# Transposing queries into (row, neighbour) order so that an output tile stores as one DMA

## The chip, the cores and the metric

The kernel runs on one core of a Trainium2 chip. The metric is the device time of one execution in microseconds (us). Each kernel was run several times beside the kernel before on the same chip. PE is the matrix engine, DVE the vector engine, ACT the scalar engine, POOL the GpSimd engine, and SP the engine that issues nearly all DMAs here.

## The reference, cut to what matters

Eight batches of 576 tokens and 8 heads of 64 go through two attentions (32 packed queries gather from k and v; then every token attends to the 32 packed rows), and the result through a two-layer block with a squared ReLU.

```python
def _attn_ref(q, k, v, p):
    p_packed = sm_attn(p, k, v)            # (8, 8, 32, 64)
    return sm_attn(q, p_packed, p_packed)  # (8, 8, 576, 64)

def _moe_ref(x, w_in, w_out):              # x: 4608 tokens x 512
    r = np.maximum(x @ w_in, 0.0)          # d_ff = 2048
    return (r * r) @ w_out                 # 4608 x 512, float32
```

One thing about checking: in the reference's own output the spread among the rows of one batch is below 1e-10 beside a typical value of 2.2e-5, because the inputs are small and the second softmax is nearly uniform. A kernel that stores rows in exchanged places therefore still compares as correct. Where an order of rows is called right below, that rests on the index arithmetic, not on the comparison.

## The kernel before

The 576 tokens of a batch are written as s = 18·a + j, with a = 0..31 (the row) and j = 0..17 (the neighbour). A load puts (head, a) on the partitions and (j, d) in the free dimension, so each partition reads one long run. DVE transposes blocks of 32 x 32; the columns of `qT`, which are the tokens from here to the end, come out in the order (j, a).

```python
def tr_q(self, qd):
    self.tile_of("qT", att, [P, NQD, 2, S], BF16, bufs=1)
    nc.vector.transpose(
        self.qT[:, qd].rearrange("p dh (j a) -> p j dh a", a=32),
        self.t.qb[qd][:].rearrange("p (j dh dl) -> p j dh dl", dh=2, dl=32))
...
def n_mul(self, qd, hf):           # softmax weights times 1/sum, on DVE
    nc.vector.tensor_tensor(out=self.a2[:, qd, n0:n1]..., in0=self.e2[qd, hf], in1=self.rs[qd, hf], op=ALU.mult)
...
def f2_out(t, eng):                # 128 tokens of output, t = 0..35
    ob[t] = opool.tile([P, NE], F32, name="o_sb")      # 3 buffers
    cast(eng, ob[t], po[t])
    for i in range(4):
        b, j = divmod(t * 4 + i, JT)                   # JT = 18
        dst = out[b * S:(b + 1) * S, :].rearrange("(a j) e -> j a e", j=JT)[j]
        nc.sync.dma_start(dst, ob[t][32 * i:32 * i + 32, :])
```

A tile of 128 tokens is four j of 32 rows each, so it is stored by four DMAs of 32 runs of 2 KB.

The softmax here doesn't subtract the row's maximum and nothing guards it: scores larger than these inputs give would overflow.

## Time and profile before

| | before |
|---|---|
| time on the chip, first three runs | 274.54 us median (274.21 to 275.49) |
| span of the profiled run | 271.4 us |
| PE / DVE / ACT / POOL busy | 243.0 / 172.7 / 168.6 / 82.7 us |
| stores | 144 of 64 KB, 1.7 us from issue to landing |

From the profile's page, kernel before: busy time of two engines, the 40 slices of DVE and PE, the DMA packets by size, and the chain that ended last.

```profile
PE 243.0 (90%) x1840; PEld 135.4 (50%) x1840; DVE 172.7 (64%) x325; ACT 168.6 (62%) x302; POOL 82.7 (30%) x127
...
PE   0436967999989999999999999999999999999992
...
DVE  4756799999949899859768974976266504510000
...
DMA packets 31129, 46.99 MB, mean 173 GB/s; under 512 B 10113, under 2 KB 18305, under 8 KB 31105
...
PE ps_o L636 31%; PE ps_h L612 17%; DVE gT L627 6%; DMA v_f<-in_v_dram 4%; DMA kq_f<-in_k_dram 4%; DMA out_dram<-o_sb 3%; DVE qT L455 3%; PE ps_a L542 3%; PE ps_s L572 3%; SPq L645 3%; PE ps_a L473 2%; DVE a L600 2%; PE ps_pp L507 2%; DVE M L552 2%; ACT o_sb L340 1%
```

Each digit of the slices is a busy share in tenths over 6.8 us. DVE is full from slice 6 to 11, PE nearly so from slice 8 on. The same as a table by stretches of time (start:end, length, then busy us and number of instructions of PE, weight loads, DVE, ACT, POOL, the PE clock that the chip granted as a share of full speed, the DMA share and GB/s):

```profile
55.00:76.00 21.00, 19.85 (x119) 11.34 (x117) 21.00 (x29) 12.19 (x21) 13.07 (x16) 1.00 1.03 260
76.00:105.00 29.00, 28.71 (x269) 15.65 (x268) 23.86 (x45) 22.15 (x44) 20.05 (x37) 1.00 0.96 271
105.00:150.00 45.00, 44.88 (x396) 27.11 (x396) 35.88 (x71) 36.09 (x67) 18.05 (x28) 1.00 0.68 193
150.00:200.00 50.00, 50.00 (x415) 28.37 (x413) 33.15 (x69) 37.40 (x69) 5.22 (x4) 1.00 0.28 73
```

From 55 to 76 us DVE has no idle time at all; after it PE has next to none, while DVE is idle for a fifth to a third.

The groups of transposes by shape (count, busy us, mean ns of one, idle before): the query transpose, and the two of the keys.

```profile
L455 DVE STREAM_TRANSPOSE qT<-q_b 128x1152 bf16<-128x1152 bf16 x16 | 21.4, 1358 | 0.4 <-ACT q_b L340 0.4
L461 DVE STREAM_TRANSPOSE kT<-k_b 128x1024 bf16<-128x1024 bf16 x16 | 19.8, 1235 | 5.7 <-PE ps_a L487 4.8 <-POOL k_b L342 0.6
L464 DVE STREAM_TRANSPOSE kT<-k_b 128x128 bf16<-128x128 bf16 x16 | 4.3, 269 | 0.0
```

From the two key transposes a column costs (1235 - 269) / (1024 - 128) = 1.08 ns, and one instruction about 0.13 us besides.

The end of the kernel: ACT's copy of the last tile and SP's four store issues.

```profile
266.65 0.59 ACT L340 COPY o_sb<-ps_o 128x512 f32<-128x512 f32 x1 [2.87 <-DMA out_dram<-o_sb]
267.26 1.73 SPq L645 DMA_DIRECT2D out_dram<-o_sb  x4
```

### The profile page before, as it was taken

Reading aid. Unit: us, or ns where it says so; the run is one execution under the profiler, and the core shown is the slowest. Engines: PE = TensorE matmul, PEld = TensorE weight load, DVE = VectorE, ACT = ScalarE, POOL = GpSimd, SP = SyncE. Lnnn points to the kernel's source line nnn. Section 1 sums busy time; section 2 is a strip of 40 time slices with the busy share of each in tenths; the row PEclk is TensorE's granted clock in tenths of the full one; section 3 lists DMA queues with packets and bytes.
Section 4 is the critical chain, followed back from the end, with each engine's and each line's share of the span. In section 5 each row is a group of like instructions: output and inputs, shape, how many; then the busy total and the mean of one; then the engine's idle time right before and its main releaser. Section 6 shows DMA issues by size and latency. Waiting matters only on the chain.

```text
span 271.4 us, 5108 instructions
## 1 busy us (share of the span) xinstructions
PE 243.0 (90%) x1840; PEld 135.4 (50%) x1840; DVE 172.7 (64%) x325; ACT 168.6 (62%) x302; POOL 82.7 (30%) x127
## 2 busy tenths in 40 slices
PE   0436967999989999999999999999999999999992
PEld 0322443456555544665565466556546646644441
DVE  4756799999949899859768974976266504510000
ACT  3436646867548798788868975976587717821110
POOL 5432338629589381362246213000000000000000
PEclk9999999999999999999999999999999999999997
DMA  7999999999897999807955911111111131113223
GB/s 258 230 310 398 270 319 386 358 261 334 176 291 236 259 330 239 332 1 168 328 173 119 280 41 40 41 39 42 39 41 39 39 77 41 40 50 76 73 74 77
DMA packets 31129, 46.99 MB, mean 173 GB/s; under 512 B 10113, under 2 KB 18305, under 8 KB 31105
## 3 DMA queue, kind: packets, MB, share of 16 engines
q1 hardware_dynamic: 30576, 46.55, 60.5%
q8 instruction: 14, 0.23, 0.4%
q10 hardware_dynamic: 528, 0.13, 0.2%
q14 instruction: 11, 0.08, 0.1%
HBM read 37.22 MB, written 9.44 MB: 172 GB/s over the span
## 4 chain that ended last, share of the span: by engine, by line
PE 60%; DVE 18%; DMA 11%; SPq 4%; ACT 2%; issue 2%; POOL 1%; DVEq 0%; POOLq 0%; ACTq 0%
PE ps_o L636 31%; PE ps_h L612 17%; DVE gT L627 6%; DMA v_f<-in_v_dram 4%; DMA kq_f<-in_k_dram 4%; DMA out_dram<-o_sb 3%; DVE qT L455 3%; PE ps_a L542 3%; PE ps_s L572 3%; SPq L645 3%; PE ps_a L473 2%; DVE a L600 2%; PE ps_pp L507 2%; DVE M L552 2%; ACT o_sb L340 1%
## 5 line engine op out<-in xcount | busy, mean ns | idle before, releaser
L636 PE MATMUL ps_o<-w_out_b,gT 128*128 128x512 bf16 x576 | 147.5, 379 | 0.4 <-DVE w_out_b L342 0.3
L620 ACT ACTIVATE r<-ps_h 128x576 bf16<-128x576 f32 x124 | 78.2, 651 | 26.6 <-PE ps_h L612 18.9
L627 DVE TENSOR_TENSOR gT<-r 128x576 bf16<-128x576 bf16 x128 | 71.1, 580 | 28.6 <-ACT r L620 27.7
L612 PE MATMUL ps_h<-a,M 128*128 128x288 bf16 x512 | 82.1, 292 | 2.2 <-DVE r L622 1.2
L636 PEld LDWEIGHTS <-gT 128*128 128x128 bf16 x576 | 54.6, 98 | 50.2 <-issue 4.4
L612 PEld LDWEIGHTS <-M 128*128 128x128 bf16 x512 | 49.7, 99 | 31.6 <-issue 6.1
L340 ACT COPY o_sb<-ps_o 128x512 f32<-128x512 f32 x29 | 17.0, 585 | 32.5 <-DMA out_dram<-o_sb 25.8
L550 ACT ACTIVATE M<-ps_a,rD 128x512 bf16<-128x512 f32 x39 | 26.4, 686 | 6.2 <-PE ps_a L542 5.8
L342 POOL CAST q_b<-kq_f 128x1152 bf16<-128x1152 f32 (+1 forms) x16 | 19.7, 1244 | 25.5 <-DMA kq_f<-in_q_dram 25.2
L342 POOL CAST v_b<-v_f 128x1280 bf16<-128x1280 f32 (+1 forms) x15 | 18.8, 1279 | 27.1 <-PE ps_pp L511 10.1
L461 DVE STREAM_TRANSPOSE kT<-k_b 128x1024 bf16<-128x1024 bf16 x16 | 19.8, 1235 | 5.7 <-PE ps_a L487 4.8
L342 POOL CAST k_b<-kq_f 128x1152 bf16<-128x1152 f32 (+1 forms) x15 | 17.7, 1180 | 13.5 <-DMA kq_f<-in_k_dram 9.4
L455 DVE STREAM_TRANSPOSE qT<-q_b 128x1152 bf16<-128x1152 bf16 x16 | 21.4, 1358 | 0.4 <-ACT q_b L340 0.4
L552 DVE TENSOR_SCALAR M<-ps_a,rD 128x512 bf16<-128x512 f32 x25 | 18.7, 747 | 4.4 <-PE ps_a L542 4.2
L473 PE MATMUL ps_a<-pT_bd,kT 128*128 128x128 bf16 x128 | 10.0, 230 | 11.0 <-DVE pT_bd L342 8.3
L542 PE MATMUL ps_a<-w_in_b,ppT 64*32 64x512 bf16 x256 | 16.8, 413 | 3.0 <-ACT M L550 1.1
L342 POOL COPY pT_bd<-pT 32x64 bf16<-32x64 bf16 x56 | 13.5, 267 | 10.9 <-PE ps_a L487 8.8
L473 PEld LDWEIGHTS <-kT 128*128 128x128 bf16 x128 | 8.6, 103 | 13.4 <-DVE kT L461 9.2
L579 ACT ACTIVATE e<-ps_s,rD 128x576 bf16<-128x576 f32 x16 | 11.4, 739 | 5.8 <-PE ps_s L572 5.7
L342 DVE CAST pq_bd<-ps_pp 32x64 bf16<-32x64 f32 x32 | 7.0, 218 | 11.2 <-PE ps_pp L511 5.9
L572 PE MATMUL ps_s<-qT,pq_bd 128*128 128x288 bf16 x64 | 11.0, 306 | 3.1 <-ACT pq_bd L340 1.8
L600 DVE TENSOR_TENSOR a<-e,rs 128x576 bf16<-128x576 bf16 x16 | 13.6, 848 | 0.0
(51 smaller groups left out, 145.0 us busy)
## 6 DMA issues: line engine op xcount, KB each, us to landing
kq_f<-in_k_dram SPq DMA_DIRECT2D x16, 576.0 KB, 8.2
kq_f<-in_q_dram SPq DMA_DIRECT2D x16, 576.0 KB, 7.1
out_dram<-o_sb SPq DMA_DIRECT2D x144, 64.0 KB, 1.7
v_f<-in_v_dram SPq DMA_DIRECT2D x28, 256.0 KB, 5.9
w_f<-in_moe_w_in_dram SPq DMA_DIRECT2D x8, 512.0 KB, 8.2
w_f<-in_moe_w_out_dram SPq DMA_DIRECT2D x8, 512.0 KB, 8.4
v_f<-in_v_dram SPq DMA_DIRECT2D x8, 128.0 KB, 6.7
v_f<-in_v_dram SPq DMA_DIRECT2D x14, 64.0 KB, 5.9
```

The source lines that it names most:

```text
L340: nc.scalar.copy(dst, src)
L342: eng.tensor_copy(dst, src)
L455: nc.vector.transpose(self.qT[:, qd].rearrange("p dh (j a) -> p j dh a", a=32), self.t.qb[qd][:].rearrange("p (j dh dl) -> p j dh dl", dh= ...
L461: nc.vector.transpose(self.kT[:, qd, :, :GM * P].rearrange("p dh (g jp a) -> p jp g dh a", jp=4, a=32), self.t.kb[qd][:, :JM * D].rearrang ...
L473: nc.tensor.matmul(ps[:, g * P:(g + 1) * P], lhsT=self.kT[:, qd, dh, g * P:(g + 1) * P], rhs=pT_bd[self.b % 2][:, (qd * 2 + dh) * P:(qd * ...
L542: nc.tensor.matmul(pss[qd][o:o + 32, :], lhsT=self.ppT[64 * e:64 * e + 64, qd, pr, :], rhs=w_in_b[64 * e:64 * e + 64, qd * 2 + pr, c * WCH ...
L550: nc.scalar.activation(dst, self.psm[c][e], ACT.Copy, scale=self.rD[:, e:e + 1])
L552: nc.vector.tensor_scalar_mul(dst, self.psm[c][e], self.rD[:, e:e + 1])
L612: nc.tensor.matmul(ps[:, c, :HALF], lhsT=a.M[:, qd, fb * FB:(fb + 1) * FB], rhs=a.a2[:, qd, c * HALF:(c + 1) * HALF], start=(qd == 0), sto ...
L620: nc.scalar.activation(dst, src, ACT.Relu)
L627: eng.tensor_tensor(out=gT[:, fb, o:o + S], in0=r, in1=r, op=ALU.mult)
L636: nc.tensor.matmul(po[t], lhsT=gT[:, fb, n0:n0 + P], rhs=w_out_b[:, fb, :], start=(fb == 0), stop=(fb == NFB - 1))
```

## The change

The columns of `qT` are to come out as (row, neighbour): four neighbours j..j+3 of row a side by side. Then four consecutive partitions of an output tile are four consecutive rows of the output, and a tile can go out as one DMA of 256 KB in runs of 8 KB. Because 18 is not a multiple of 4, a pair of neighbours is left per batch; it stands at the end of even batches and at the start of odd ones, and a tile that crosses from one batch to the next is stored in two halves. PE sees the same columns in another order.

```diff
             def tr_q(self, qd):
                 self.tile_of("qT", att, [P, NQD, 2, S], BF16, bufs=1)
-                nc.vector.transpose(
-                    self.qT[:, qd].rearrange("p dh (j a) -> p j dh a", a=32),
-                    self.t.qb[qd][:].rearrange("p (j dh dl) -> p j dh dl", dh=2, dl=32))
+                j0 = 2 * (self.b % 2)
+                parts = (j0, 4, j0 * 32), (j0 - 2 if j0 else 16, 2, 0 if j0 else 4 * P)
+                for j, w, c in sorted(parts):
+                    n = 16 if w == 4 else 2
+                    nc.vector.transpose(
+                        self.qT[:, qd, :, c:c + n * 32].rearrange("p dh (t a w) -> p t w dh a", a=32, w=w),
+                        self.t.qb[qd][:, j * D:(j + n) * D].rearrange("p (t w dh dl) -> p t w dh dl", w=w, dh=2, dl=32))
...
-            for i in range(4):
+            i = 0
+            while i < 4:
                 b, j = divmod(t * 4 + i, JT)
-                dst = out[b * S:(b + 1) * S, :].rearrange("(a j) e -> j a e", j=JT)[j]
-                nc.sync.dma_start(dst, ob[t][32 * i:32 * i + 32, :])
+                n = min(4 - i, JT - j)
+                dst = out[b * S:(b + 1) * S, :].rearrange("(a j) e -> a j e", j=JT)[:, j:j + n]
+                nc.sync.dma_start(dst, ob[t][32 * i:32 * (i + n), :])
+                i += n
```

In the first part the innermost output dimension `a` now has a stride of w = 4 columns, that is 8 B, and in the small part of 2 columns, 4 B. Before, it was contiguous.

## The prediction

> What bounds it now. The stretch table shows three stages. From 35 to 76 us DVE is busy 40.4 of 41 us and the chain of waits runs through it. From 76 to 246 us PE is nearly always busy (idle 0.3 us until 105, then about 0.1), so PE work sets the end. The tail from 246 us is six output tiles, one per 3.46 us: 16 matmuls at the 216 ns that unbroken runs of this line show earlier in the chain, so PE again. The chain says ACT waits there for an output DMA (25.8 us in 9 waits), but there are three output buffers and a store lands 1.6–1.7 us after issue, so I read these as coincidence: PE's last matmul of the tile ends at the same moment. After PE's end (266.6 us) come one copy (0.59 us), four store issues (267.3 to 268.6 us), one landing (1.65 us); the span ends at 271.4.
>
> What goes. 144 stores of 64 KB become 40 (36 tiles, four cut in two at a batch boundary): 104 issues of 0.42 us, 44 us of SP queue time. SP mostly waits for its inputs after 105 us, so that is off the chain. From 60 to 105 us, eight stores in a row hold the queue 7.4 us ahead of the v loads, which will now land earlier; the chain holds no load after 33 us: 0 to -0.3 us. In the tail one issue replaces four: the last starts 1.3 us earlier. Its 256 KB take longer: at the 300 GB/s that loads reach here the extra 192 KB take 0.6 us (estimate). Net -0.7 us. This wants 16 engines per store: the Trainium skill, "DMA: Bandwidth & Descriptors", section "Why a DMA increments its semaphore by 16 and not by 1", takes the largest divisor up to 16 of both sides' slowest dimensions, here 32 and 128, so 16. Today's stores agree (482 packets under 512 B for 30 stores in the tail: 16 completions each).
>
> What comes. Each query transpose (16 of 1152 columns, 1.36 us, one per 1.30 us back to back) becomes two, of 1024 and 128. The key transposes have these sizes: 1.245 and 0.269 us, a pair per 1.35 us. So +0.05 us each, 0.8 us of DVE in all; five lie in the DVE-bound beginning, two more on the chain near 100 us: +0.3 us. New too: output is written at a stride of 8 B (4 B in the small part). The skill, "SBUF — State Buffer", section "Door 1: The DMA port swizzle", gives 16-byte lines that want at least two hits each; 8 B gives just two. No transpose of this trace writes so; I assume 1.09 ns per column stays. PE work and the order of instructions do not change.
>
> Sum: -0.7 + 0.3 = -0.4 us: 274.2 us, range 272.8 to 276.0. Chances: faster by over 2% 0.03, within 2% 0.92, slower by over 2% 0.05.
>
> What would show it. Query transposes of about 1.25 and 0.27 us; 40 stores landing in about 2.2 us; PE full from 76 us on, tail tiles still 3.46 us apart though ACT's wait for stores is gone or renamed; 4.1 us from PE's end to the span's end, in place of 4.8.
>
> What would make it wrong. Strided writes at half rate: +1.2 us per transpose, some 8 us on the chain, 3% slower. ACT truly waiting for the previous tile's stores in the tail: tiles come faster than 3.46 us. A large store on few engines: its landing takes several us. Earlier loads speeding up POOL work that feeds PE near 75 us: up to 1 us gained.

## More of the kernel before

A small planner in the kernel fixes the order of the instructions on each engine from assumed costs; it takes 1.38 us for a query transpose.

A piece of DVE's timeline in the middle of the kernel (start us, us, what): the work of one batch around its two query transposes.

```profile
123.60 0.75 DVE L552 TENSOR_SCALAR M<-ps_a,rD 128x512 bf16<-128x512 f32 x1
124.27 1.19 DVE L627 TENSOR_TENSOR gT<-r 128x576 bf16<-128x576 bf16 x2
125.38 2.62 DVE L455 STREAM_TRANSPOSE qT<-q_b 128x1152 bf16<-128x1152 bf16 x2
127.93 0.71 DVE L600 TENSOR_TENSOR a<-e,rs 128x576 bf16<-128x576 bf16 x1
128.57 0.73 DVE L552 TENSOR_SCALAR M<-ps_a,rD 128x512 bf16<-128x512 f32 x1
```

From one M to the next are 4.97 us. M is what DVE (at other times ACT) makes of a block of `ps_a`, and PE's next matmuls into `ps_a` wait for it.

## The result, and the profile after

| | before | after |
|---|---|---|
| time | 274.38 us median (272.93 to 275.49, 4 runs) | 285.82 us median (285.58 to 288.63, 4 runs) |
| ratio | | 1.0476, 95% interval 1.0401 to 1.0551: slower |
| span of the profiled run | 271.4 us | 283.9 us |
| DVE busy | 172.7 us | 188.4 us |
| stores | 144, 1.7 us to landing | 40, 2.4 us to landing |

A ratio is the mean time of one kernel's runs over the mean of the other's in the same rounds, so it is not quite the ratio of the medians.

The page's lines again, kernel after. Lines of the source have moved by 4 to 6 (L455 is now L459, L636 is L640, L645 is L651).

```profile
PE 244.3 (86%) x1810; PEld 135.6 (48%) x1840; DVE 188.4 (66%) x341; ACT 169.1 (60%) x302; POOL 82.9 (29%) x127
...
PE   0537866999789897999799989989999999999993
...
DVE  4777899999939999859967993897347522520000
...
DMA packets 29464, 46.98 MB, mean 166 GB/s; under 512 B 8448, under 2 KB 16640, under 8 KB 29440
...
PE ps_o L640 29%; PE ps_h L616 14%; DVE qT L459 12%; DVE gT L631 8%; DVE M L556 4%; DVE kT L465 4%; DMA v_f<-in_v_dram 2%; DVE a L604 2%; PE ps_a L477 2%; DVE pq_bd L342 2%; PE ps_a L546 2%; DMA kq_f<-in_q_dram 1%; PE ps_s L576 1%; DVE ppT L342 1%; ACT pq_bd L340 1%
```

The query transposes have gone from 3% to 12% of the chain, and PE's row now has holes (7 or 8) up to slice 27. The packets are worth a look too. There are 1,665 fewer, which is, within one, the 104 stores saved times 16 completions, all under 512 B. The packets between 2 and 8 KB are 31105 - 18305 = 12,800 before and 29440 - 16640 = 12,800 after. So the runs of 8 KB in the output made no larger packets. The tile still has 2 KB per partition on its own side.

The same stretches and the same groups, kernel after:

```profile
55.00:76.00 21.00, 19.86 (x118) 11.53 (x119) 21.00 (x26) 11.61 (x20) 10.25 (x9) 1.00 1.06 273
76.00:105.00 29.00, 25.12 (x227) 13.62 (x229) 23.15 (x46) 18.10 (x38) 23.12 (x44) 0.94 0.79 244
105.00:150.00 45.00, 41.33 (x339) 23.98 (x342) 37.42 (x63) 33.44 (x59) 11.80 (x16) 1.00 0.60 178
150.00:200.00 50.00, 46.87 (x387) 27.57 (x393) 40.10 (x76) 37.49 (x68) 11.36 (x16) 1.00 0.30 85
```

```profile
L459 DVE STREAM_TRANSPOSE qT<-q_b 128x1024 bf16<-128x1024 bf16 x16 | 38.8, 2422 | 0.0
L465 DVE STREAM_TRANSPOSE kT<-k_b 128x1024 bf16<-128x1024 bf16 x16 | 19.8, 1235 | 5.9 <-PE ps_a L491 5.6
L459 DVE STREAM_TRANSPOSE qT<-q_b 128x128 bf16<-128x128 bf16 x16 | 5.2, 328 | 0.0
L468 DVE STREAM_TRANSPOSE kT<-k_b 128x128 bf16<-128x128 bf16 x16 | 4.3, 269 | 0.0
```

A query transpose of 1024 columns now takes 2.42 us where the key transpose of exactly that size takes 1.24. Both move the same bytes; what differs is the stride of the output (the ladder in e4 varies it alone). PE, which had 0.1 us of idle time in 105 to 200 us, now has 3.67 + 3.13 = 6.8.

The timeline around the two query transposes of one batch, kernel after, and two of PE's waits, over the whole span, before (first two lines) and after (engine, what, released by: us in all, times, longest):

```profile
131.15 0.75 DVE L556 TENSOR_SCALAR M<-ps_a,rD 128x512 bf16<-128x512 f32 x1
131.82 1.19 DVE L631 TENSOR_TENSOR gT<-r 128x576 bf16<-128x576 bf16 x2
132.93 5.10 DVE L459 STREAM_TRANSPOSE qT<-q_b 128x128 bf16<-128x128 bf16 x4
137.84 0.78 DVE L604 TENSOR_TENSOR a<-e,rs 128x576 bf16<-128x576 bf16 x1
138.53 0.72 DVE L556 TENSOR_SCALAR M<-ps_a,rD 128x512 bf16<-128x512 f32 x1
```

```profile
PE ps_a L542 <- DVE M L552: 0.2, 1, 0.2
PE ps_s L572 <- DVE qT L455: 1.3, 1, 1.3
...
PE ps_a L546 <- DVE M L556: 6.4, 5, 1.6
PE ps_s L576 <- DVE qT L459: 4.3, 3, 2.4
```

From M to M are now 7.38 us in place of 4.97. From the first transpose to the multiply behind it are 4.91 us in place of 2.55, so one query block costs (4.91 - 2.55) / 2 = 1.18 us more, some 19 us for all 16. (I go by the distance of starts. On the page the transposes' own busy time grows by 19.6 us, from 21.4 to 41.0, but DVE's total by 15.7 us only; the durations of neighbours overlap and do not simply add up.) PE has work for about the old distance and then waits for M: the idle time that DVE has on average in this stretch is not in front of M.

The end, kernel after:

```profile
279.61 0.59 ACT L340 COPY o_sb<-ps_o 128x512 f32<-128x512 f32 x1 [2.87 <-PE ps_o L640]
...
L651 SPq DMA_DIRECT2D out_dram<-o_sb x1: 539/539/539, 280.2 to 280.2; - x1
```

Tiles still come 3.45 us apart at the end, and ACT's wait there is now put down to PE, as the prediction expected of a coincidence.

To see where the 12.5 us of span come in, I read off when the copies of output tiles start: the copy of the first tile (0), of tile 8, of the last (35), and the end of the span. This table has the runs of the experiments below too.

| profiled run | tile 0 at | 0 to 8 | 8 to 35 | 35 to end |
|---|---|---|---|---|
| before | 59.01 | 50.15 | 157.49 | 4.75 |
| before again (e13) | 61.88 | 51.76 | 157.50 | 4.76 |
| **after** | 60.02 | 56.69 | 162.90 | 4.29 |
| new order, old stores (e1) | 61.27 | 54.77 | 162.71 | 4.75 |
| old order, new stores (e14) | 60.83 | 49.30 | 157.50 | 4.27 |
| new stores, first half (e9) | 59.87 | 50.13 | 157.49 | 5.21 |
| new stores, second half (e10) | 60.24 | 49.42 | 157.49 | 4.45 |
| contiguous transposes twice (e8) | 63.34 | 57.54 | 165.85 | 4.77 |
| pairs (e5) | 61.42 | 48.56 | 157.43 | 4.79 |
| order in the multiply (e7) | 58.72 | 50.76 | 158.54 | 4.28 |
| pairs of pairs (e12) | 62.10 | 50.94 | 157.31 | 4.25 |

The stretch from tile 8 to 35 repeats to a hundredth of a microsecond between two runs of the kernel before. The first two columns do not: tile 0 comes anywhere between 59.0 and 61.9 us in kernels that are alike up to there (before, e9, e10, e13, e14), often with a lower granted PE clock between 35 and 60 us (0.83 in the mean of 35 to 55 us for e10, 1.00 for before). After against before: +1.0 us until tile 0, +6.5 from 0 to 8, +5.4 from 8 to 35, -0.5 at the end, together 12.5. Of these the first two carry a spread of 2 to 3 us, the last two next to none. Part of the 6.5 may be the granted clock: from 76 to 105 us it was 0.94 in the kernel after, 1.00 in before and in e1, and e1 took 54.77 us for this stretch.

### The profile page after: what moved, and what is told of

Read it like the earlier page. It is cut to its first block, busy times and chain, and to the rows that moved or that the text cites. A ratio compares the mean times of both kernels' runs of the same rounds, so it can differ in the third digit from the quotient of the medians.

```text
span 283.9 us, 4949 instructions
## 1 busy us (share of the span) xinstructions
PE 244.3 (86%) x1810; PEld 135.6 (48%) x1840; DVE 188.4 (66%) x341; ACT 169.1 (60%) x302; POOL 82.9 (29%) x127
## 2 busy tenths in 40 slices
DMA packets 29464, 46.98 MB, mean 166 GB/s; under 512 B 8448, under 2 KB 16640, under 8 KB 29440
## 4 chain that ended last, share of the span: by engine, by line
PE 50%; DVE 37%; DMA 4%; issue 4%; POOL 1%; ACT 1%; SPq 1%; ACTq 0%; DVEq 0%
PE ps_o L640 29%; PE ps_h L616 14%; DVE qT L459 12%; DVE gT L631 8%; DVE M L556 4%; DVE kT L465 4%; DMA v_f<-in_v_dram 2%; DVE a L604 2%; PE ps_a L477 2%; DVE pq_bd L342 2%; PE ps_a L546 2%; DMA kq_f<-in_q_dram 1%; PE ps_s L576 1%; DVE ppT L342 1%; ACT pq_bd L340 1%
## 5 line engine op out<-in xcount | busy, mean ns | idle before, releaser
L640 PE MATMUL ps_o<-w_out_b,gT 128*128 128x512 bf16 x546 | 142.2, 382 | 1.8 <-DVE gT L631 0.4
L640 PEld LDWEIGHTS <-gT 128*128 128x128 bf16 x576 | 54.7, 98 | 50.9 <-issue 4.8
L459 DVE STREAM_TRANSPOSE qT<-q_b 128x1024 bf16<-128x1024 bf16 (+1 forms) x32 | 41.0, 1375 | 0.1
L342 POOL CAST q_b<-kq_f 128x1152 bf16<-128x1152 f32 (+1 forms) x16 | 19.0, 1199 | 26.9 <-DMA kq_f<-in_q_dram 18.1
L546 PE MATMUL ps_a<-w_in_b,ppT 64*32 64x512 bf16 x256 | 18.4, 413 | 8.3 <-DVE M L556 6.4
L546 PEld LDWEIGHTS <-ppT 64*32 64x32 bf16 x256 | 4.8, 90 | 23.4 <-issue 19.0
```

The source lines that it names most:

```text
L342: eng.tensor_copy(dst, src)
L459: nc.vector.transpose(self.qT[:, qd, :, c:c + n * 32].rearrange("p dh (t a w) -> p t w dh a", a=32, w=w), self.t.qb[qd][:, j * D:(j + n) * ...
L546: nc.tensor.matmul(pss[qd][o:o + 32, :], lhsT=self.ppT[64 * e:64 * e + 64, qd, pr, :], rhs=w_in_b[64 * e:64 * e + 64, qd * 2 + pr, c * WCH ...
L640: nc.tensor.matmul(po[t], lhsT=gT[:, fb, n0:n0 + P], rhs=w_out_b[:, fb, :], start=(fb == 0), stop=(fb == NFB - 1))
```

## The experiments

Theory A: the transposes became slow through the stride of their output, and this DVE time is the whole loss. Rivals: B, the new stores cost it; C, strided writes hurt other engines through the memory, beyond their own duration. Then: what rule gives the price of a stride, and is there a way to have the new stores without it?

### e1: the new order alone

```diff
 # tr_q as in the kernel after, f2_out as in the kernel before
```

> The new query transposes alone, with the four old stores per tile (its rows come out in the wrong places, on purpose). Theory A, the slower transposes are the whole loss: about 286 us, query transposes again 2.42 and 0.33 us, PE idle again for some 10 us between 76 and 200 us. Rival B, the new stores cost it: about 274.5 us.

Measured: 286.67 us median of three runs (285.46 to 289.15; a fourth, slow, took 289.77), ratio 1.0475 (1.0411 to 1.0538). The transposes took 2.42 and 0.32 us:

```profile
L459 DVE STREAM_TRANSPOSE qT<-q_b 128x1024 bf16<-128x1024 bf16 x16 | 38.8, 2424 | 0.3 <-ACT q_b L340 0.3
```

The table shows 162.71 us from tile 8 to 35 and the old 4.75 us at the end. The whole loss is in `tr_q`. B falls.

### e2 and e14: the new stores alone, twice

```diff
 # tr_q as in the kernel before, f2_out as in the kernel after (rows in wrong places, on purpose)
```

> The new stores alone, with the old contiguous query transposes (wrong rows, on purpose). Theory A: 273.5 to 274.4 us, that is 0 to 0.3% faster than the kernel before, from PE's end to the end of the span 4.4 us in place of 4.85 us. Rival B: about 286 us.

> The new stores alone once more. The traces show what they can do only after the first store at 60 us: about 1 us between the third and the ninth tile, and 0.4 us at the end. If that is all: ratio 0.994 to 0.996. If the earlier 1.1% was real: 0.989.

Measured: e2 272.65 us (median of five runs of six), ratio 0.9886 (0.9839 to 0.9933); its profiled run was slow, so its trace is not used. e14: 274.45 us, ratio 0.9998 (0.9951 to 1.0045). It was run at another time. The first 1.1% did not come again. In e14's trace 0.48 us are gained at the end (4.27 against 4.75) and nothing from tile 8 to 35. The stores cost nothing and gain about half a microsecond that can be shown; a further gain of up to some 1 us in the stretch from tile 0 to 8 is inside the spread there.

### e9 and e10: the new stores in one half of the tiles

```diff
+            if t < 18:        # e9; e10 has t >= 18
+                ... the new stores
+                return
             for i in range(4):
```

> New stores for tiles 0 to 17 only, old for the rest, old transposes (rows of the first half in wrong places, on purpose). The new stores alone gained 1.1%, more than the 0.7 us of the tail that the prediction counted. If the rest came from the stretch where stores and loads share the queue: ratio 0.990 to 0.995 here. If it is all at the end: 1.000.

> The complement: new stores for tiles 18 to 35 only. By the tail alone 0.4 to 0.7 us less, ratio 0.997 to 0.9985. If the 1.1% sat here: 0.989.

Measured: e9 0.9916 (0.9842 to 0.9990); e10 0.9970 (0.9927 to 1.0013). Taken alone, e9's ratio says that the gain is early. But it rests on three of six runs (270.48, 271.56 and 274.48 us): the other three, 274.85 to 275.50, count as slow only because they lie over 1.5% above the fastest, and leaving them out lowers the mean. Over all six runs the mean is 273.71 us, 0.996 of the kernel before over all of its runs. Nor does e9's trace show the gain: from tile 0 to 8 it takes 50.13 us with the new stores, and e10 takes 49.42 us with the old ones there. So the early gain stays unproven.

### e13: the kernel before as its own candidate

> The kernel before, unchanged, as if it were a candidate: ratio 1.000, and its interval shows how far 0.989 and 0.998 of other runs can be trusted. By the spread so far it may lie anywhere from 0.995 to 1.005.

Measured: 1.0021 (0.9966 to 1.0076), five runs from 273.95 to 277.86 us (a sixth, slow, took 278.74). Differences of half a per cent can't be told by these runs, and e2's 1.1% with its own tight interval shows that even 1% deserves a second look here.

### e8: the same amount of DVE time without any stride

```diff
                 nc.vector.transpose( ... contiguous ... )
+                nc.vector.transpose( ... the same once more ... )
```

> The kernel before with each contiguous query transpose simply done twice: 16 more of 1.36 us, about 21 us more DVE time, no strided write, old stores, right result. Theory A, it is plain DVE time at this place of the order that costs: the after kernel added 18 us of transpose time for 11.4 us, so this adds about 13 us, 285 to 290 us. Rival C, strided writes hurt the other engines' use of the memory: then plain DVE time costs clearly less, under 280 us.

Measured: 292.85 us, ratio 1.0655 (1.0592 to 1.0718); 16 more transposes of 1.36 to 1.38 us. The expectation of A was too low by 3 us in size, but C falls: plain contiguous DVE time at this place costs no less than the strided one, and PE waits for M in its trace too (7.4 us from 105 to 200 us, against 5.7 in the kernel after and 0.2 before). About 21 us more gave 18 us; the 19 us of the change gave 13. The relation is steeper than a straight line through zero. That a first part of each delay is absorbed by slack would give this, but it is not shown: e8's profiled run also had a lower granted clock (0.973 on average against 0.994 in the kernel after).

### e4: a ladder of strides

```diff
+                if self.b == 0: nc.vector.transpose(*at(1, 0, 18))      # 2 B
+                elif self.b == 1: nc.vector.transpose(*at(2, 0, 18))    # 4 B
+                ...                                                     # 6, 8, 12, 16, 18, 36 B, one line each
```

> Each batch's query transposes write at another stride: 2, 4, 6, 8, 12, 16, 18, 36 B (columns end in the wrong order, on purpose; only the durations count). Known so far: 2 B 1.36 us per 1152 columns, 8 B 2.42 us per 1024. Theory S1, cost grows with the number of 16-byte lines that a run of 32 columns touches (4, 8, 12, 16, 24, 32, 32, 32): about 1.8 us at 4 B, 2.3 at 6 B, 3.6 at 12 B, and 4.5 us from 16 B on. Theory S2, one step up once the stride is not contiguous and flat from there: about 2.7 us per 1152 columns for 8, 12, 16, 18 and 36 B alike. Theory S3, bank conflicts: 8 and 16 B slower than 6, 12, 18 and 36 B.

Measured (one run of unknown state, 311.26 us, with two transposes for each stride; only the durations are used, and its 2.46 us at 8 B is near the 2.42 us of the fast runs). Groups by line, which here means by stride: 2, 4, 6, 8, 12, 16, 18 and 36 B. Columns: count, minimum/median/maximum ns, first and last start.

```profile
L459 DVE STREAM_TRANSPOSE qT<-q_b x2: 1378/1378/1379, 10.6 to 19.0; 128x1152 bf16<-128x1152 bf16 x2
L461 DVE STREAM_TRANSPOSE qT<-q_b x2: 1414/1441/1468, 47.6 to 49.0; 128x1152 bf16<-128x1152 bf16 x2
L463 DVE STREAM_TRANSPOSE qT<-q_b x2: 2064/2073/2082, 71.9 to 73.8; 128x1152 bf16<-128x1152 bf16 x2
L465 DVE STREAM_TRANSPOSE qT<-q_b x2: 2457/2462/2468, 88.4 to 91.5; 128x1024 bf16<-128x1024 bf16 x2
...
L468 DVE STREAM_TRANSPOSE qT<-q_b x2: 4004/4031/4058, 103.2 to 107.8; 128x1152 bf16<-128x1152 bf16 x2
L470 DVE STREAM_TRANSPOSE qT<-q_b x2: 4644/4697/4750, 135.1 to 139.9; 128x1024 bf16<-128x1024 bf16 x2
...
L473 DVE STREAM_TRANSPOSE qT<-q_b x2: 5274/5336/5397, 167.3 to 172.2; 128x1152 bf16<-128x1152 bf16 x2
L475 DVE STREAM_TRANSPOSE qT<-q_b x2: 5143/5216/5289, 201.9 to 206.6; 128x1152 bf16<-128x1152 bf16 x2
```

Take off 0.13 us for the instruction, divide by the columns, and count the 16-byte lines that 32 columns of one run touch:

| stride | 2 B | 4 B | 6 B | 8 B | 12 B | 16 B | 18 B | 36 B |
|---|---|---|---|---|---|---|---|---|
| ns per column | 1.08 | 1.14 | 1.69 | 2.28 | 3.39 | 4.46 | 4.52 | 4.41 |
| lines per 32 columns | 4 | 8 | 12 | 16 | 24 | 32 | 32 | 32 |
| ns per line | 8.7 | 4.6 | 4.5 | 4.6 | 4.5 | 4.5 | 4.5 | 4.4 |

The price is about 4.5 ns per line visited, with a floor of 1.08 ns per column. It grows with the stride up to 16 B and is flat from there on, as lines of 16 bytes would have it. S1 holds in its shape, with this floor in place of my straight line: 4 B is nearly free (I had expected 1.8 us). S2 and S3 fall: it neither levels off at 8 B, nor do 8 and 16 B stand out from 6, 12 and 18 B.

### e7: the new order made in a multiply

```diff
-                nc.vector.tensor_tensor(out=self.a2[:, qd, n0:n1]..., in0=e2, in1=rs, op=ALU.mult)
+                for j, w, c in sorted(parts):      # parts as in the kernel after
+                    n = (16 if w == 4 else 2) * 32
+                    nc.vector.tensor_tensor(
+                        out=self.a2[:, qd, c:c + n].rearrange("p (t a w) -> p t w a", a=32, w=w),
+                        in0=e[:, j * 32:j * 32 + n].rearrange("p (t w a) -> p t w a", a=32, w=w),
+                        in1=r[:, j * 32:j * 32 + n].rearrange("p (t w a) -> p t w a", a=32, w=w), op=ALU.mult)
 # old tr_q, new stores
```

> Old contiguous query transposes; the new order is made where the softmax weights are multiplied by 1/sum (DVE, 576 columns, 0.75 us when undisturbed), written at the same 8 B stride in 512 columns; new stores; right result. If the price [...] per 16-byte line holds for every strided bf16 write of DVE: these take about 1.2 us for 512 columns plus 0.2 for 64, +0.6 us each, 9 us in all, and the time is 276 to 280 us. If it belongs to the transpose alone: 0.65 plus 0.15 us and about 272 to 274 us.

Measured: 275.28 us, ratio 1.0027 (0.9962 to 1.0092), below the range of the first and above that of the second. The durations decide. Both multiplies of a block, and what follows them, in DVE's timeline of this run:

```profile
128.26 1.33 DVE L605 TENSOR_TENSOR a<-e,rs 128x512 bf16<-128x512 bf16 x2
129.48 0.70 DVE L552 TENSOR_SCALAR M<-ps_a,rD 128x512 bf16<-128x512 f32 x1
```

They take 1.22 us to the next start, where the one multiply before took 0.64 (127.93 to 128.57), that is 1.11 ns per column, near the floor of the transpose. By the line rule 512 columns at 8 B visit 256 lines: 256 x 4.5 ns = 1.15 us, plus 0.07 us for the 64 columns. So the price isn't special to the transpose. It is paid on half as many columns here, +0.58 us per block, and much of it disappears into slack: +1.05 us from tile 8 to 35.

### e5: pairs of neighbours

```diff
+                nc.vector.transpose(
+                    self.qT[:, qd].rearrange("p dh (t a w) -> p t w dh a", a=32, w=2),
+                    self.t.qb[qd][:].rearrange("p (t w dh dl) -> p t w dh dl", w=2, dh=2, dl=32))
...
+            for i in (0, 2):     # two stores of 128 KB, runs of 4 KB
```

> Neighbours in pairs instead of fours: one transpose per query block that writes at a 4 B stride, and two stores of 128 KB in 4 KB runs per tile; right result. The ladder had 1.44 us at 4 B against 1.36-1.38 contiguous, so DVE gains 16 x 0.07 = 1.1 us only. If the stores alone are worth the 1.1% of the earlier run, and the 4 B stride is nearly free in place too: 271 to 273.5 us, ratio 0.988 to 0.995. Rival: if a strided write hurts through more than its own duration, it stays at 275 us or above.

Measured: 274.06 us, ratio 0.9981 (0.9930 to 1.0032), transposes 1.45 us. So a strided write whose line visits fit into the floor (8 lines per 32 columns: about 36 ns of visits against 35 ns of floor) costs nothing that can be seen: 157.43 us from tile 8 to 35. The end takes 4.79 us, so two stores of 128 KB gain nothing there.

### e12: the full order in two cheap steps

```diff
 # tr_q in pairs as in e5; new stores; the multiply writes runs of two columns at an 8 B stride
+                for i in range(2):
+                    nc.vector.tensor_tensor(
+                        out=o4.rearrange("p (t a v w) -> p t v a w", a=32, v=2, w=2)[:, :, i],
+                        in0=e4.rearrange("p (t v a w) -> p t v a w", a=32, v=2, w=2)[:, :, i], ...)
```

> The full order (row, four neighbours) in two cheap steps: transposes at a 4 B stride, then the multiply writes runs of two columns at an 8 B stride (two multiplies of 256 columns and one of 64 per block); the new stores of 256 KB; right result. If the price is per visit to a 16-byte line, four columns fall into each visit and the 256-column multiplies take 0.35 to 0.4 us; if it is the price of an 8 B stride as such, 0.6 us. Time by the first: 272 to 274 us, ratio 0.992 to 0.998; by the second some 4 us more of DVE, of which about a quarter shows.

Measured: the undisturbed multiplies of 256 columns took 396 to 416 ns (minimum and median), and two of them 0.66 us to the next start:

```profile
131.57 0.74 DVE L605 TENSOR_TENSOR a<-e,rs 128x256 bf16<-128x256 bf16 x2
132.23 0.74 DVE L552 TENSOR_SCALAR M<-ps_a,rD 128x512 bf16<-128x512 f32 x1
```

The price is that of visits to lines, not of the 8 B step. The time was 276.44 us, ratio 1.0069 (1.0032 to 1.0105), so the expected gain did not come. Its trace has 157.31 us from tile 8 to 35 and 4.25 at the end, as good as any, but tile 0 at 62.10. The granted clock was 0.83 from 35 to 55 us in that run, and the extra DVE instructions fall into the stretch where DVE is full; how much either of them did was not separated.

### e11: the kernel after, with the planner told the true cost

```diff
-            us = 1.45 if nm == "k" else 1.38
+            us = 1.45 if nm == "k" else 2.55
```

> The after kernel, but the planner that fixes each engine's order is told 2.55 us for a query transpose in place of 1.38; same instructions, another order; right result. If the later part of the loss (8.5 of 13 us after tile 4) is misplacement, slow transposes standing in front of work that PE waits for while DVE still has idle time: 277 to 281 us. If it is DVE throughput everywhere: 284 to 286 us.

Measured: 283.67 us median of three runs (280.54 to 284.32; a fourth, slow, took 285.84), ratio 1.0301 (1.0231 to 1.0371): between the two expectations, about a third of the loss regained. The stretches of the profiled run, its fastest:

```profile
76.00:105.00 29.00, 25.26 (x236) 13.71 (x234) 24.28 (x46) 22.25 (x43) 16.86 (x26) 0.88 0.82 239
105.00:150.00 45.00, 44.50 (x375) 25.33 (x373) 35.97 (x68) 35.44 (x67) 18.41 (x28) 1.00 0.62 189
150.00:200.00 50.00, 49.86 (x407) 29.10 (x406) 36.10 (x66) 36.81 (x65) 4.75 (x4) 1.00 0.27 76
```

PE's idle time from 105 to 200 us is 0.6 us in place of 6.8, and no wait for a DVE-made M is left in it. So there the loss was a matter of place: DVE had the time, but the transposes stood in front of M. I expected 277 to 281 us from this, having put the regainable part at 8.5 us, that is everything after tile 4. The profiled run did regain that: from tile 4 to tile 35 it takes 183.3 us, the kernel after 194.3, the kernel before 185.8. But tile 4 itself comes at 91.2 us, in place of 85.3 in after and 80.9 in before: the new order lost time early, and PE idles 3.7 us from 76 to 105 us at a granted clock of 0.88. How much of this is the order and how much the clock was not separated.

None of the kernels that store every row in its place is clearly faster than the kernel before. The nearest, e5, has an interval that holds 1.

## Why the prediction was wrong, point by point

- **The step that failed** is "I assume 1.09 ns per column stays". The 8 B stride cost 2.28 ns per column, so a block takes 1.18 us more, not 0.05, and DVE got some 19 us more, not 0.8. The prediction had drawn on the Trainium skill, "SBUF — State Buffer", section "Door 1: The DMA port swizzle", where two hits per 16-byte line suffice. The runs show otherwise: about four bf16 columns per visit are needed (e4, e12). The trace of the kernel before could not decide it, and the prediction said so, but gave it 5%. e1 and e2/e14 show that this step is the whole of the loss.
- **The case named as what would make it wrong** was right in its mechanism: "Strided writes at half rate: +1.2 us per transpose". It measured 1.18. Its sum, "some 8 us on the chain, 3% slower", was too low: 13 us. It counted the seven transposes that stood on the chain of the kernel before. The nine others were not on it; with 2.4 us more per batch the slack that DVE had there no longer covered them, and PE came to wait for M (6.4 us against 0.2): 5.4 us were lost from tile 8 to 35, where PE had been full. The e11 run shows those waits to be a matter of place.
- **"PE full from 76 us on"** failed for that reason: 6.8 us idle from 105 to 200 us.
- **The tail.** "Net -0.7 us" measured -0.46 (4.75 to 4.29 us, one store in place of four), and the same in e14. The mechanism was right. The landing took 2.4 us in place of the expected 2.2, and the issue 0.54 in place of 0.42.
- **16 engines per store** is consistent with the trace: 1,665 fewer packets is 104 x 16 within one packet, so each remaining store still has 16 completions. This agrees with the Trainium skill, "DMA: Bandwidth & Descriptors", section "Why a DMA increments its semaphore by 16 and not by 1".
- **ACT's wait for stores** at the end was a coincidence, as predicted: with new stores it is put down to PE, and the tiles stay 3.45 us apart.
- **Earlier loads** ("0 to -0.3 us"): no gain beyond the spread could be shown. The queue time saved bought nothing that could be shown beyond the tail. It was some 39 us (144 issues of 0.42 us against 40 of 0.54, an estimate from the medians), not the predicted 44, which left out that an issue became longer.

## What to carry to other kernels

Before a layout change trades DMA count for a strided write, count how many 16-byte lines each run visits: on this DVE a visit cost about 4.5 ns, so bf16 in steps of 4 B, or in runs of two columns every 8 B (four columns per line in both cases), were nearly free, and single columns every 8 B doubled the time. An engine's average idle time is no allowance for a longer instruction; ask what stands behind that instruction in the fixed order and who waits for it. And a gain of 1% from one set of runs can vanish in the next: run the old kernel as its own candidate first.

## What the Trainium skill lacked or had wrong

- "SBUF — State Buffer", section "Door 1: The DMA port swizzle": says at least two hits per 16-byte line give full bandwidth, and that bf16 can stride by up to 8 elements for free. For DVE writes of bf16, 8 B (two hits) cost 2.28 ns per column and 16 B 4.46, against 1.08 contiguous; only 4 B (four hits) was nearly free at 1.14.
- "VectorE: DVE Perf Modes", section "Mode 1× (REGULAR) — the baseline": says that weird strides work in this mode at one result per cycle, and names no price for them. A multiply of the same 576 columns took 1.22 us with 512 of them written at 8 B, against 0.64 contiguous. No trace shows the mode; one operand of this multiply is float32, and contiguous it took 1.11 ns per column.
- No page that I read says what a store does whose two sides have runs of different length. Runs of 8 KB in the output with 2 KB per partition in the tile gave the same 12,800 packets of 2 to 8 KB as runs of 2 KB; only the completions became fewer (1,665).
